# A filter product moved into an earlier slot of the interleaved order, and two of a unit's four closing sums moved one turn later

## The chip, the cores and the metric

The kernel runs on one core of a Trainium2 chip. The metric is device time in microseconds of one execution; the runs of the kernel before gave 2632.1, 2633.94 and 2633.98 us, median 2633.94.

## What is computed

A real FFT along the sequence, a product with a complex filter, the inverse FFT, and then a two-layer block with an ELU between the layers. Everything is float32.

```python
batch, seq, dim = (8, 3008, 256);  n_tokens, d_model, d_ff = (24064, 256, 2048)
X = np.fft.rfft(x, axis=1)
Y = X * (filt_r + 1j * filt_i)[None, :, :]
x = np.fft.irfft(Y, n=3008, axis=1).reshape(24064, 256)
h = x @ w_in
g = np.where(h > 0.0, h, np.exp(np.minimum(h, 0.0)) - 1.0)
return g @ w_out
```

## The kernel before

**Two workloads in one order.** The length 3008 is 47 x 64, and the FFT is done as products with small tables. Batch 0 goes through its FFT in a first stage (about the first 105 us of the span). From then on the two-layer block of batch b-1 and the FFT of batch b share the engines: the two-layer block is the base load, and the FFT's steps are put between its steps at places written out by hand.

**The two-layer block.** The tokens of a batch are cut into six units, m = 0 to 5 (512 tokens each, 448 for m = 0). The hidden width is cut into four, q = 0 to 3. One item is (batch, m, q): 192 items in all. Both matrix products of an item are made with seven block products instead of eight (a Strassen-like scheme), so that sums on VectorE stand around them. The main loop (lines 948 to 970) has one *turn* per item: turn i issues the seven "up" steps of item i (`up_steps`, line 515: x @ w_in and the ELU) interleaved with the seven "down" steps of item i-1 (`down_steps`, line 600: g @ w_out into the four PSUM tiles po0 to po3). A step is two matmuls in the program, which the profile shows as four instructions. The up steps go in the order 1, 2, 6, 5, 7, 3, 4 (`UPS`).

Four lines of the up steps matter here:

```python
def s7():
    add("b22", mm(7, "d", True), g["t4"])     # VectorE reads bank phd
...
def s4():
    add("b21", mm(4, "d", False), g["t2"])    # TensorE adds onto the same bank phd
```

Step 7 writes the PSUM bank phd, VectorE reads it in the sum "b22" (line 538), and only then may step 4 add onto the same bank. Two other steps (3, and one down step) lie between steps 7 and 4 on TensorE. In the profile step 7 is `phd<-y`, step 4 is `phd<-ys`, both at line 530, and "b22" is the first `g<-phd` of a turn at line 538. The sum "b11" is the one `g<-pha` of a turn.

**Places in a turn.** `at(turn, place, fn)` fills a plan. Place 2 stands after the third step of a turn, place 0 in the middle (after the seventh or eighth step), place 1 at the end, behind the closing sums of the turn's up item (lines 588 to 592) and, where q is 3, behind three sums of the down item (line 628). Each engine works its instructions in program order.

**The FFT of batch b** has its turns counted from t = 24(b-1); r below is the turn's number less t. Four input steps `x_unit` (four VectorE operations for a pair, lines 219 and 220) stand in place 0 of r = 0, 2, 4 (for b = 1: 2, 3, 4). Then four groups follow, with s = t + 6, 10, 14, 18: `b_unit` at s, `re_mult` and `re_sums` at s+1, `im_mult` and `im_join` at s+2 (r = 8, 12, 16, 20), `im_sums` and `bi_unit` at s+3 (r = 9, 13, 17, 21). `im_mult` (line 415) makes four 128x512 products for the filter, lines 417 and 418, once for c = 0 and once for c = 1; `im_join` (line 423) adds them; `im_sums` (line 428) makes two sums that the matmuls of `bi_unit` (line 445) read. The filter's next slices are read by `f_read` (line 323, issued by GpSimd), which waits for the last `im_mult` of the group before. `n_unit` (line 479), TensorE work that makes the two-layer block's next input, stands in place 0 of r = 8, 12, 16 and 23 and in place 1 of r = 1 and 5; r = 20 has none. The four sums behind it, `n_sums` (lines 505 to 508), stand at the end of r = 1, 5, 9, 13 and 17 and in place 0 of r = 23.

**A unit's end.** When q = 3 is done, ScalarE copies po0 and po1 (line 617), VectorE makes three sums in the turn's tail, and a list `rest` of four more sums, all at line 628, runs in `c_unit`, place 0 of r = 4m + 5. One turn later, in place 0 of r = 4m + 6, `o_unit` makes two transposes on VectorE (line 650) and issues the output's DMAs on SyncE (line 660). So `c_unit` falls on r = 5, 9, 13, 17, 21 and 25, and `o_unit` on r = 6, 10, 14, 18, 22 and 26; r = 26 is r = 2 of the next batch, whose `x_unit` pair stands in the same place behind it.

Of the kernel before, what the change touches and what calls it, by code (L numbers as in the profile page):

```python
# [130 lines left out]
def kernel(  # L131
# [51 lines left out]
    xs, tas, tns, t1s, t2s, rs, ss, t3s, t4s, zs, yds, ys, g_of, po_of, cs_, sds = ({} for _ in range(16))  # L183

    def raw(src, row, ap, col=0):
        return bass.AP(tensor=src.tensor, offset=src.offset + row * D + col, ap=ap)
# [281 lines left out]
    def half(m):  # L468

        return 224 if m == 0 else 256  # L470
# [129 lines left out]
    def down_steps(b, m, q):  # L600
        h = half(m)
        g = g_of.pop((b, m, q))
        if q == 0:
            po_of[b, m] = [psO.tile([P, 2, 256], FP32, tag="po%d" % i, name="po%d" % i) for i in range(4)]
        po = po_of[b, m]
        k = {}

        def step(n):
            i, u = PLACE[n]
            for a in range(2):  # L610

                nc.tensor.matmul(po[i][:, u, 0:h], w_out[q][:, COMBO[n], a, :], g[n][:, a, :],  # L612
                                 start=q == 0 and a == 0 and n in (1, 3, 6, 4), stop=True, skip_group_check=True)
            if q == 3 and n == 7:
                for i in range(2):
                    t = k[i] = kp.tile([P, 2, 256], FP32, tag="k%d" % i, name="k%d" % i)
                    nc.scalar.activation(out=t[:, :, 0:h], in_=po[i][:, :, 0:h], func=AXT.Copy)

        def tail():
            if q != 3:  # L620
                return
            p1, p5 = (k[0][:, u, 0:h] for u in range(2))
            p35, p7 = (k[1][:, u, 0:h] for u in range(2))
            c = kp.tile([P, 2, 512], FP32, tag="c", name="c")
            (c11, c12), (c21, c22) = ((c[:, i, 0:h], c[:, i, h:2 * h]) for i in range(2))

            def add(o, i0, i1):
                nc.vector.tensor_tensor(out=o, in0=i0, in1=i1, op=ALU.add)  # L628

            add(p35, p35, p5)  # L630
            add(c12, po[2][:, 1, 0:h], p1)
            add(c11, po[2][:, 0, 0:h], p1)
            rest = [(p7, p7, c12), (c12, c12, p35), (c21, po[3][:, 0, 0:h], p7), (c22, p7, p5)]
            cs_[b, m] = c, lambda: [add(*r) for r in rest]

        return [(lambda n=n: step(n)) for n in DOWNS], tail

# [2 lines left out]


    def c_unit(b, m):
        cs_[b, m][1]()

    def o_unit(b, m):
        c, _ = cs_.pop((b, m))
        o = op.tile([P, 16, 2, 32], FP32, tag="o", name="o")
        n = 7 if m == 0 else 8
        for k in range(2):
            nc.vector.transpose(out=o.rearrange("p (j k) e s -> p j k e s", k=2)[:, 0:n, k],  # L650
                                in_=c.rearrange("p e (j k s) -> p j k e s", k=2, s=32)[:, 0:n, k])

        o = o.rearrange("p (u f k) e s -> p u f k (e s)", u=4, f=2)
        queues = itertools.cycle((nc.sync, nc.scalar) if (b, m) == (B - 1, 5) else (nc.sync,))
        for k in range(2):
            for u, w, i in ((0, 3, 1), (3, 1, 0)) if m == 0 else ((0, 4, 4 * m),):
                for f in range(1 if i == 0 else 2):
                    n1 = N1 - i if f else i
                    for a in range(4):
                        next(queues).dma_start(raw(out, b * N + n1 + 32 * N1 * k,  # L660
                                                   [[N1 * D, 32], [-D if f else D, w], [1, 64]], 64 * a),
                                               o[ts(a, 32), u:u + w, f, k])
# [113 lines left out]
    with tc.manual_schedule():  # L776
# [118 lines left out]
        def at(quad, place, fn, *a):  # L895
            plan.setdefault((quad, place), []).append((fn, a))
# [13 lines left out]
        for b in range(B):  # L910
            t = (b - 1) * PER
            if b > 0:
                for c, s in enumerate((2, 2, 3, 3, 4, 4) if b == 1 else (0, 0, 2, 2, 4, 4)):
                    at(t + s, 0, x_unit, b, c)
                    if c % 2 == 0:
                        opens.add(t + s + 1)
                        at(t + s, 1, a_unit, b, c)
                    nb, nxt = (b, c + XBUFS) if c + XBUFS < NXC else (b + 1, c + XBUFS - NXC)
                    if nb < B:
                        at(t + s, 1, x_load, nb, nxt)  # L920
                    at(t + s, 1, z_write, b, c)
                for g in range(0, NG, 2):
                    s = t + 6 + 2 * g
                    opens.update((s + 1, s + 4))
                    for k in (g, g + 1):
                        at(s - 2, 1, f_read, b, k)
                        at(s - 1, 0, z_read, b, k)
                    at(s, 1, b_unit, b, g)
                    at(s + 1, 2, re_mult, b, g)
                    at(s + 1, 1, re_sums, b, g)  # L930
                    at(s + 2, 2, im_mult, b, g, 0)
                    at(s + 2, 1, im_mult, b, g, 1)
                    at(s + 2, 1, im_join, b, g)
                    at(s + 3, 2, im_sums, b, g)
                    at(s + 3, 1, bi_unit, b, g)
                    at(s + 3, 1, y_write, b, g)
            for m, (s, place) in enumerate(((23, 0), (25, 1), (29, 1), (32, 0), (36, 0), (40, 0))):
                if b > 0 or m > 0:
                    at(t + s - 2, 0, tn_read, b, m)
                    at(t + s - 2, 1 if m == 0 else 0, y_read, b, m)  # L940
                    at(t + s, place, n_unit, b, m)

                    at(*((t + s + 1, 1) if m > 2 else (t + s, place)), n_sums, b, m)
                at(t + PER + 4 * m + 5, 0, c_unit, b, m)
                at(t + PER + 4 * m + 6, 0, o_unit, b, m)

        items = [(b, m, q) for b in range(B) for m in range(6) for q in range(4)]
        for i in range(-PER, len(items) + 3):
# [3 lines left out]
            for n, k in enumerate("DUUDUDDU" if i in opens else "UUDUDDU"):  # L952
                s = ups if k == "U" else downs
# [7 lines left out]
            for k in "DUUDUD" if i in opens else "DUUDUDD":  # L961
                s = ups if k == "U" else downs
# [40 lines left out]
```

## Time and profile before

| what | value |
|---|---|
| median of the runs | 2633.94 us |
| the profiled execution | 2636.78 us |
| its span, first to last instruction | 2635.0 us |
| granted TensorE clock, mean | 0.992 |
| TensorE busy | 2556.2 us, 97% |
| VectorE busy | 2041.0 us, 77% |
| ScalarE busy | 1549.3 us, 59% |
| GpSimd busy | 166.2 us, 6% |
| VectorE line 628 | 288 sums, median 415 to 425 ns |
| VectorE lines 417, 418 | 56 products each, mean 691 and 683 ns |
| VectorE line 650 | 96 transposes, median 670 ns |

Time in the tables is of one profiled execution. "Busy" is the union of an engine's instructions. In a timeline's line, the first number is the start in us from the span's start, the second the duration, then engine, line, operation, out<-in and shapes; a bracket gives the idle time in front of it and what ended that. On VectorE the next instruction can start before the one in front has its end on record (starts 0.60 us apart for durations of 0.68), so costs on VectorE are taken from start to start. Matmuls overlap in the same manner: four of a step start 0.2 us apart though each is recorded with 0.38 us.

### The profile page before, as it was taken

Reading aid. Unit: us, or ns where it says so; the run is one execution under the profiler, and the core shown is the slowest. Engines: PE = TensorE matmul, PEld = TensorE weight load, DVE = VectorE, ACT = ScalarE, POOL = GpSimd, SP = SyncE. Lnnn points to the kernel's source line nnn. Section 1 sums busy time; section 2 is a strip of 40 time slices with the busy share of each in tenths; the row PEclk is TensorE's granted clock in tenths of the full one; section 3 lists DMA queues with packets and bytes.
Section 4 is the critical chain, followed back from the end, with each engine's and each line's share of the span. In section 5 each row is a group of like instructions: output and inputs, shape, how many; then the busy total and the mean of one; then the engine's idle time right before and its main releaser. Section 6 shows DMA issues by size and latency. Waiting matters only on the chain.

```text
span 2635.0 us, 39708 instructions
## 1 busy us (share of the span) xinstructions
PE 2556.2 (97%) x14460; PEld 2202.1 (84%) x14460; DVE 2041.0 (77%) x3538; ACT 1549.3 (59%) x2713; POOL 166.2 (6%) x333
## 2 busy tenths in 40 slices
PE   5799999999999999999999999999999999999998
PEld 4588879888898888988889888898888888798887
DVE  6878887788777887777877888778887788866666
ACT  6665555665556555655556555565555655555554
POOL 5100000001000100000000000000000000000000
PEclk8899999999999999999999999999999999999999
DMA  9562213522243232433215231253213322120010
GB/s 290 160 173 70 57 37 94 129 57 69 49 117 82 69 73 48 109 86 72 65 41 140 70 84 39 65 130 81 60 38 89 83 68 57 39 58 20 21 29 17
DMA packets 228834, 206.37 MB, mean 78 GB/s; under 512 B 130962, under 2 KB 194674, under 8 KB 228640
## 3 DMA queue, kind: packets, MB, share of 16 engines
q1 hardware_dynamic: 211328, 166.87, 25.8%
q0 software_dynamic: 15856, 36.25, 4.9%
q8 instruction: 114, 1.87, 0.3%
q10 hardware_dynamic: 1456, 0.72, 0.1%
q14 instruction: 80, 0.66, 0.1%
HBM read 131.87 MB, written 78.17 MB: 80 GB/s over the span
## 4 chain that ended last, share of the span: by engine, by line
PE 77%; DVE 15%; ACT 3%; issue 2%; DMA 0%; DVEq 0%; ACTq 0%
PE po L612 34%; PE phs L530 20%; PE phd L530 10%; PE pha L530 5%; PE psn L479 3%; DVE g L538 2%; DVE g L552 2%; DVE c L628 2%; PE psa L233 1%; PE pf L382 1%; DVE zs L428 1%; PE pv L445 1%; ACT e L548 1%; ACT e L547 1%; DVE g L589 1%
## 5 line engine op out<-in xcount | busy, mean ns | idle before, releaser
L612 PE MATMUL po<-g,wo 128*128 128x256 f32 (+1 forms) x5376 | 1313.4, 376 | 0.0
L612 PEld LDWEIGHTS po<-g,wo 128*128 128x128 f32 x5376 | 1013.1, 190 | 162.2 <-issue 47.4
L541 ACT ACTIVATE g<-phs 128x512 f32<-128x512 f32 (+1 forms) x576 | 338.6, 588 | 763.4 <-PE phs L530 763.3
L538 DVE TENSOR_TENSOR g<-phd,g 128x512 f32<-128x512 f32 (+1 forms) x384 | 259.6, 676 | 346.2 <-ACT e L548 228.5
L548 ACT ACTIVATE e<-e 128x512 f32<-128x512 f32 (+1 forms) x768 | 477.2, 621 | 24.3
L547 ACT ACTIVATE e<-g 128x512 f32<-128x512 f32 (+1 forms) x576 | 354.1, 615 | 84.9 <-DVE g L538 47.8
L530 PE MATMUL phs<-y,wi 128*128 128x256 f32 (+1 forms) x1536 | 389.3, 376 | 0.5
L530 PE MATMUL phs<-ys,wi 128*128 128x256 f32 (+1 forms) x1536 | 387.8, 375 | 1.5 <-ACT g L541 1.5
L552 DVE SCALAR_TENSOR_TENSOR g<-e,g 128x512 f32<-128x512 f32 (+1 forms) x576 | 387.4, 673 | 1.7 <-ACT e L548 0.2
L530 PEld LDWEIGHTS phs<-ys,wi 128*128 128x128 f32 x1536 | 291.7, 190 | 35.0 <-ACT g L541 2.2
L530 PEld LDWEIGHTS phs<-y,wi 128*128 128x128 f32 x1536 | 287.9, 190 | 38.4 <-ACT fall L390 3.4
L552 DVE SCALAR_TENSOR_TENSOR g<-e,phs 128x512 f32<-128x512 f32 (+1 forms) x192 | 129.7, 676 | 124.9 <-ACT e L548 124.9
L530 PE MATMUL phd<-ys,wi 128*128 128x256 f32 (+1 forms) x768 | 197.5, 380 | 28.7 <-DVE g L538 28.1
L530 PE MATMUL pha<-y,wi 128*128 128x256 f32 (+1 forms) x768 | 193.9, 375 | 0.0
L530 PE MATMUL phd<-y,wi 128*128 128x256 f32 (+1 forms) x768 | 193.8, 375 | 0.0
L530 PEld LDWEIGHTS phd<-ys,wi 128*128 128x128 f32 x768 | 143.0, 190 | 57.5 <-DVE g L538 42.6
L547 ACT ACTIVATE e<-phs 128x512 f32<-128x512 f32 (+1 forms) x192 | 112.8, 587 | 109.3 <-PE phs L530 109.3
L323 POOL DMA_DIRECT2D fall<-fp x224 | 110.0, 499 | 836.8 <-DVE r L418 775.1
L530 PEld LDWEIGHTS pha<-y,wi 128*128 128x128 f32 x768 | 146.3, 191 | 16.5
L530 PEld LDWEIGHTS phd<-y,wi 128*128 128x128 f32 x768 | 146.0, 190 | 16.4
L538 DVE TENSOR_TENSOR g<-pha,g 128x512 f32<-128x512 f32 (+1 forms) x192 | 129.2, 673 | 25.4 <-PE pha L530 25.3
L589 DVE TENSOR_TENSOR g<-g,g 128x512 f32<-128x512 f32 (+1 forms) x192 | 130.7, 681 | 6.7
(138 smaller groups left out, 2119.2 us busy)
## 6 DMA issues: line engine op xcount, KB each, us to landing
yd<-t SPq DMA_DIRECT2D x127, 192.0 KB
t<-yd SPq DMA_DIRECT2D x190, 128.0 KB
z<-t SPq DMA_DIRECT2D x84, 256.0 KB
fall<-fp POOLq DMA_DIRECT2D x224, 96.0 KB, 3.0
t<-z SPq DMA_DIRECT2D x224, 96.0 KB
out_dram<-o SPq DMA_DIRECT2D x632, 32.0 KB
tn<-tn_t SPq DMA_DIRECT2D x48, 256.0 KB
xc<-in_x_dram SPq DMA_DIRECT2D x84, 128.0 KB
```

What stands on the lines that cost most here:

```text
L233: nc.tensor.matmul(p[o:o + 64, u, :], w[r, u, o:o + 64], src[r, u, :], start=True, stop=True)
L323: nc.gpsimd.dma_start(t[32 * a:32 * a + 24].rearrange("p c u d -> p (c u d)"), fp[g, a].rearrange("q c u d -> q (c u d)"))
L479: nc.tensor.matmul(ps[:, ts(q, P)], t[:, i - 4 * m, ds(dh * P, P)], w[:, i - 4 * m, :], start=True, stop=True)
L530: nc.tensor.matmul(ps[:, a, 0:h], w_in[q][:, COMBO[n], a, :], y[n], start=start and a == 0, stop=True, skip_group_check=True)
L538: nc.vector.tensor_tensor(out=g[o], in0=i0, in1=i1, op=ALU.add)
L541: nc.scalar.activation(out=g[o], in_=i0, func=AXT.Copy)
L547: nc.scalar.activation(out=e, in_=src, func=AXT.Relu, scale=-1.0)
L548: nc.scalar.activation(out=e, in_=e, func=AXT.Exp, scale=-1.0)
L552: nc.vector.scalar_tensor_tensor(out=g[n], in0=es[n], scalar=1.0, in1=src, op0=ALU.subtract, op1=ALU.max)
L589: nc.vector.tensor_tensor(out=b12, in0=b22, in1=b12, op=ALU.subtract)
L612: nc.tensor.matmul(po[i][:, u, 0:h], w_out[q][:, COMBO[n], a, :], g[n][:, a, :], start=q == 0 and a == 0 and n in (1, 3, 6, 4), stop=True, ...
L628: nc.vector.tensor_tensor(out=o, in0=i0, in1=i1, op=ALU.add)
```

## The change

The list `rest` has its second and third sum exchanged, and is run in two halves: (p7, c21) stays in `c_unit`, and (c12, c22) goes to the start of `o_unit`, one turn later, in front of the transposes. `im_mult` for c = 1 moves from place 1 of its turn (the end) to place 2 (behind the third step), directly behind `im_mult` for c = 0. No instruction is added or dropped.

```diff
-            rest = [(p7, p7, c12), (c12, c12, p35), (c21, po[3][:, 0, 0:h], p7), (c22, p7, p5)]
-            cs_[b, m] = c, lambda: [add(*r) for r in rest]
+            rest = [(p7, p7, c12), (c21, po[3][:, 0, 0:h], p7), (c12, c12, p35), (c22, p7, p5)]
+            cs_[b, m] = c, lambda i: [add(*r) for r in rest[i:i + 2]]
...
     def c_unit(b, m):
-        cs_[b, m][1]()
+        cs_[b, m][1](0)
 
     def o_unit(b, m):
-        c, _ = cs_.pop((b, m))
+        c, join = cs_.pop((b, m))
+        join(2)
         o = op.tile([P, 16, 2, 32], FP32, tag="o", name="o")
...
-                    at(s + 2, 2, im_mult, b, g, 0)
-                    at(s + 2, 1, im_mult, b, g, 1)
+                    for c in range(2):
+                        at(s + 2, 2, im_mult, b, g, c)
                     at(s + 2, 1, im_join, b, g)
```

## The prediction, made before the changed kernel was run

> **What bounds the kernel now.** I read the page first, for the bound, then the list of waits, for what the bound waits for, then the timelines of TensorE and VectorE around those waits, turn by turn. Turns are named by r as above.
>
> On the page TensorE is busy 97% of the span and VectorE 77%. The page's chain of the work that ended last:
>
> ```profile
> PE 77%; DVE 15%; ACT 3%; issue 2%; DMA 0%; DVEq 0%; ACTq 0%
> ```
>
> TensorE is the bound, but 15% of the chain that ended last runs over VectorE: there are stretches in which VectorE decides when TensorE goes on. The list of waits (total us, times, longest) names the place:
>
> ```profile
> PE phd L530 <- DVE g L538: 28.1, 29, 1.4
> ```
>
> Step 4 waits for the sum b22. In the timeline of TensorE these waits are regular: in each of the seven batches 0.85 us in r = 9, 13, 17 and 1.38 us in r = 21, together 21 x 0.85 + 7 x 1.38 = 27.5 us; one of 0.6 us is left over, at 146 us. One of them, at r = 13, in TensorE's timeline:
>
> ```profile
> 1233.04 1.03 PE L530 MATMUL phd<-y,wi 128*128 128x256 f32 x4
> 1233.90 1.03 PE L530 MATMUL phs<-y,wi 128*128 128x256 f32 x4
> 1234.76 1.03 PE L612 MATMUL po<-g,wo 128*128 128x256 f32 x4
> 1236.64 1.13 PE L530 MATMUL phd<-ys,wi 128*128 128x256 f32 x4 [0.85 <-DVE g L538]
> 1237.61 1.89 PE L612 MATMUL po<-g,wo 128*128 128x256 f32 x8
> ```
>
> Steps start 0.864 us apart when nothing holds them (1233.90 to 1234.76). From 1234.76 to 1237.61 there are two steps, 1.73 us, in 2.85: the stall costs 1.12 us, more than its idle row, because overlap with the step in front is lost (0.16) and the step behind starts late too (0.11). At r = 21 the same two steps take 3.37 us (1340.84 to 1344.21): 1.64 us. VectorE in front of it, r = 12 and 13:
>
> ```profile
> 1219.95 0.68 DVE L418 TENSOR_TENSOR r<-r,fall 128x512 f32<-128x512 f32 x1
> 1222.09 0.69 DVE L538 TENSOR_TENSOR g<-phd,g 128x512 f32<-128x512 f32 x1 [1.45 <-PE phd L530]
> ...
> 1230.23 0.68 DVE L417 TENSOR_TENSOR r<-r,fall 128x512 f32<-128x512 f32 x1
> 1230.83 0.69 DVE L418 TENSOR_TENSOR r<-r,fall 128x512 f32<-128x512 f32 x1
> 1231.43 1.29 DVE L423 TENSOR_TENSOR r<-r 128x512 f32<-128x512 f32 x2
> ...
> 1234.44 0.42 DVE L628 TENSOR_TENSOR k<-k,c 128x256 f32<-128x256 f32 x1
> 1234.89 0.42 DVE L628 TENSOR_TENSOR c<-c,k 128x256 f32<-128x256 f32 x1
> 1235.23 0.42 DVE L628 TENSOR_TENSOR c<-po,k 128x256 f32<-128x256 f32 x1
> 1235.57 0.42 DVE L628 TENSOR_TENSOR c<-k,k 128x256 f32<-128x256 f32 x1
> 1235.90 0.68 DVE L538 TENSOR_TENSOR g<-phd,g 128x512 f32<-128x512 f32 x1
> ```
>
> In r = 12 VectorE idles 1.45 us in front of b22, waiting for step 7. From 1224.77 to 1235.90 it has no idle time, and b22 of r = 13 starts 2.86 us after step 7 did (1233.04). In an undisturbed turn it starts 1.135 us after step 7 (1220.95 to 1222.09), step 4 follows 2.59 us after step 7, and step 4 needs b22 0.74 us before it (1235.90 to 1236.64). So b22 may start up to 1.85 us after step 7 without any cost: that is the measure for every row below.
>
> **The product c = 1 in place 2.** It removes lines 417 and 418 from the queue ahead of r = 9, 13, 17, 21 (1230.23 to 1231.43, 1.20 us) and puts the same 1.20 us ahead of b22 in r = 8, 12, 16, 20. In r = 12 the 1.45 us of idle time covers it, and in r = 8 and 16 idle times of 1.36 and 1.45 do: cost nothing, with 0.16 us over; if the cover is gone, the slack from 1.135 to 1.85 still takes 0.7 us. r = 20 has no `n_unit` in front of step 7, and so no idle time; TensorE's timeline and then VectorE's:
>
> ```profile
> 1327.02 1.03 PE L530 MATMUL phd<-y,wi 128*128 128x256 f32 x4
> 1329.61 1.03 PE L530 MATMUL phd<-ys,wi 128*128 128x256 f32 x4
> ```
>
> ```profile
> 1327.81 0.68 DVE L418 TENSOR_TENSOR r<-r,fall 128x512 f32<-128x512 f32 x1
> 1328.41 0.68 DVE L538 TENSOR_TENSOR g<-phd,g 128x512 f32<-128x512 f32 x1
> ```
>
> b22 there starts 1.39 us after step 7 and would start 1.20 us later, at 1329.61; step 4 can then start at 1329.61 + 0.74 = 1330.35 and not at 1329.61. With the 0.11 us for the step behind, a new stall of 0.85 us, seven times: 5.9 us. The rest of r = 20 is hardly later: one of the maxima behind b22 (line 552) waits for ScalarE until 1330.78 anyway, so VectorE has caught up there, and what step 4 being late adds behind it is some 0.2 us.
>
> **The two sums one turn later.** In r = 9, 13, 17, 21 they leave the queue ahead of b22. Four sums now take 1.46 us (1234.44 to 1235.90): 0.45 for one whose successor reads its result, 0.34 for the others. The half (p7, c21) takes 0.45 + 0.34 = 0.79, so 0.67 go. In `o_unit` c12 and c22 come in front of the transposes, which read c22: 0.34 + 0.45 = 0.79 us. In r = 6, 10, 14, 18, 22 VectorE idles between 2.44 and 4.14 us in front of b22 (3.77 at 1195.57): covered. In r = 2 the `x_unit` pair stands behind the transposes, and b22 is late already (a timeline of both engines):
>
> ```profile
> 1088.77 0.62 DVE L538 TENSOR_TENSOR g<-phd,g 128x448 f32<-128x448 f32 x1
> 1089.44 1.02 PE L530 MATMUL phd<-ys,wi 128*128 128x224 f32 x4
> ```
>
> b22 has no idle time in front of it, it starts as soon as the last operation of the pair lets it (line 220, 1088.16), and step 4 starts 1.00 us after the step in front (1088.44), where 0.756 is its spacing with 224 columns. Any delay there is paid in full: 0.79 us, in the six batches (b = 2 to 7) in which the output of a unit m = 5 meets an `x_unit` pair: 4.7 us. The 13 or so output DMAs of a unit are issued on SyncE 0.79 us later as well. Behind them in SyncE's queue stand table, input and x loads for turns to come, and the list of that queue's waits shows it waiting for producers, 1002 us in line 456 alone: nothing.
>
> **One rule weighed.** A sum whose successor reads it takes 0.45 us from start to start and the others 0.34 (the four rows of line 628 above), and I use both. The Trainium skill, "VectorE: DVE Perf Modes", section "The DRAIN you can't avoid", says that a semaphore between chained VectorE operations adds nothing. By that rule c12 and c22 would cost 0.68 us in r = 2 and not 0.79, and the gain would be 0.7 us larger; the row goes against the rule, by 0.11 us, and I keep the row.
>
> **What is late next.** With both edits b22 of r = 9, 13, 17 reaches the head of VectorE's queue 2.86 - 1.20 - 0.67 = 0.99 us after step 7, before its data: it starts at 1.135, and step 4 doesn't wait. With the product alone it would be 1.66, still under 1.85. In r = 21, 3.40 - 1.20 - 0.67, less the 0.85 that TensorE is later by and plus 0.2: 0.98; also clear. The other input of b22, t4, is made by ScalarE at 1232.38 to 1232.98 in r = 13, 1.2 us before it is wanted. `f_read` on GpSimd waits for line 418 and so starts some 9 us sooner, and takes 3.9 us of descriptor work; at its place now (1231.81) the VectorE operations beside it keep 0.68 us, and its transfers land in 3.0 us, some two turns before `re_mult` reads them: nothing.
>
> **Sum.** 21 x 1.12 + 7 x 1.64 = 35.1 us of stalls go; 5.9 (r = 20) and 4.7 (r = 2) come. Net 24.4 us. From the profiled 2636.8 us (span 2635.0 and 1.8 around it) this gives 2612.4; the median of the runs is 2.8 us below the profiled one, so **2609.5 us** is forecast, 0.93% less. A measurement tells 0.2% (5.3 us) from no change.
>
> **Unknown costs and the rivals.** (a) *The stalls are only worth their idle rows.* Ends of matmuls are modelled, so the spacing may overstate what returns. Then 27.5 us go, and 7 x 0.57 (1330.35 less 1329.78, the end of the step in front) and 6 x 0.79 come: 18.7 us, 2615.2. Against it: the spacing of starts is not modelled. (b) *The new stalls don't come*, because VectorE reaches b22 sooner than its rows say: up to 35.1 us, 2599 us; r = 20 alone gone, 2603.5. Against it: both places have zero idle time on VectorE in front of b22 now. (c) *Slower.* In r = 9, 13, 17, 21 step 4 could find b22 held by its other input, t4 from ScalarE, as late as VectorE's queue makes it now; then nothing is won, and the 10.7 us of r = 20 and r = 2 are paid: 2644.6. It decides from the point at which ScalarE's copy ends 2.9 us later than it does (1232.98 to 1235.90). ScalarE is idle 2 us in front of that copy, waiting for TensorE, which speaks against it. (d) *Nothing changes*, since the sums and products reach VectorE in another order than the program's or wait for something not shown: 2634.
>
> Chances: forecast 0.76, (a) 0.12, (b) 0.07, (c) 0.03, (d) 0.02. So faster 0.95, same 0.02, slower 0.03. The range takes in (a), and of (b) the case without the stall in r = 20, with about 1.5 us on either side for the drift between runs (the runs of before differ by 1.9): 2602 to 2617.
>
> **What would show it.** The list of waits should give step 4 for b22 at about 10 us instead of 28.1: seven of 0.57 in r = 20, six of 0.9 in r = 2, the one at 146 us. At r = 13 the four steps from 7 to 4 should be evenly 0.864 apart, with b22 1.135 us after step 7; r = 20 should take 12.9 us instead of 12.1. The prediction is wrong in its mechanism if a wait of another engine stands in front of step 4 in r = 13, or of line 445 behind it, and in its sizes if r = 8, 12 or 16 stalls too.

## The result, and the profile after

The changed kernel takes 2609.81 us (median of 4 runs, 2608.95 to 2612.41) beside 2633.37 us before (4 runs): a ratio of 0.9913, 95% interval 0.9896 to 0.993. That is 23.6 us less; 2609.5 us and 24.4 us less were forecast. The profiled execution took 2609.69 us with a span of 2607.9 us.

The page's chain, and the wait of step 4 for b22 in the list of waits of the changed kernel:

```profile
PE 89%; DVE 6%; DMA 2%; ACT 1%; issue 1%; POOL 0%; DVEq 0%; ACTq 0%; POOLq 0%
```

```profile
PE phd L530 <- DVE g L538: 10.0, 14, 0.9
```

VectorE's share of the chain fell from 15% to 6%, and the wait from 28.1 us in 29 places to 10.0 us in 14: "about 10 us, seven of 0.57, six of 0.9, the one at 146 us" was the expectation. TensorE's timeline of r = 13 in the same batch as before:

```profile
1219.01 1.03 PE L530 MATMUL phd<-y,wi 128*128 128x256 f32 x4
1219.87 1.03 PE L530 MATMUL phs<-y,wi 128*128 128x256 f32 x4
1220.74 1.03 PE L612 MATMUL po<-g,wo 128*128 128x256 f32 x4
1221.60 1.03 PE L530 MATMUL phd<-ys,wi 128*128 128x256 f32 x4
1222.46 1.89 PE L612 MATMUL po<-g,wo 128*128 128x256 f32 x8
```

Steps 7 to 4 and the one behind stand 0.86 us apart with no bracket, where 1.12 us were lost. VectorE's timeline of r = 12 and 13:

```profile
1206.53 0.68 DVE L417 TENSOR_TENSOR r<-r,fall 128x512 f32<-128x512 f32 x1
1207.13 0.68 DVE L418 TENSOR_TENSOR r<-r,fall 128x512 f32<-128x512 f32 x1
1208.06 0.69 DVE L538 TENSOR_TENSOR g<-phd,g 128x512 f32<-128x512 f32 x1 [0.25 <-PE phd L530]
...
1219.21 0.41 DVE L628 TENSOR_TENSOR k<-k,c 128x256 f32<-128x256 f32 x1
1219.65 0.42 DVE L628 TENSOR_TENSOR c<-po,k 128x256 f32<-128x256 f32 x1
1220.14 0.69 DVE L538 TENSOR_TENSOR g<-phd,g 128x512 f32<-128x512 f32 x1
```

The idle time in front of b22 of r = 12 went from 1.45 to 0.25 us, by the 1.20 us of the two products, and b22 itself starts as it did, 1.13 us after step 7. In r = 13 two sums are left in front of b22, which now starts 1.13 us after step 7 (1219.01 to 1220.14) and not 2.86. The bill is in the other two places. r = 20, TensorE and then VectorE:

```profile
1310.76 1.03 PE L530 MATMUL phd<-y,wi 128*128 128x256 f32 x4
...
1314.10 1.13 PE L530 MATMUL phd<-ys,wi 128*128 128x256 f32 x4 [0.58 <-DVE g L538]
1315.07 1.89 PE L612 MATMUL po<-g,wo 128*128 128x256 f32 x8
```

```profile
1312.76 0.68 DVE L418 TENSOR_TENSOR r<-r,fall 128x512 f32<-128x512 f32 x1
1313.36 0.69 DVE L538 TENSOR_TENSOR g<-phd,g 128x512 f32<-128x512 f32 x1
```

And r = 2, in a timeline of all engines:

```profile
1071.23 0.41 DVE L628 TENSOR_TENSOR c<-c,k 128x256 f32<-128x256 f32 x1
1071.56 0.42 DVE L628 TENSOR_TENSOR c<-k,k 128x256 f32<-128x256 f32 x1
1072.01 1.30 DVE L651 STREAM_TRANSPOSE o<-c 128x512 f32<-128x512 f32 x2
...
1075.86 0.62 DVE L538 TENSOR_TENSOR g<-phd,g 128x448 f32<-128x448 f32 x1
...
1076.53 1.02 PE L530 MATMUL phd<-ys,wi 128*128 128x224 f32 x4 [0.88 <-DVE g L538]
```

In r = 20 b22 starts 2.60 us after step 7 and step 4 waits; in r = 2 the two sums take 0.33 and 0.45 us in front of the transposes, and the wait of step 4 grows from 0.09 to 0.88 us.

A turn's length, from the start of one step 1 to that of the next, gives the same account for one batch (the fourth; the others agree within 0.1 us, but for the first, whose r = 0 to 4 hold other work):

| turn r | before, us | after, us | difference |
|---|---|---|---|
| 2 | 13.79 | 14.59 | +0.80 |
| 9 | 15.49 | 14.37 | -1.12 |
| 13, 17 | 15.33 | 14.22 | -1.11 each |
| 20 | 12.09 | 12.94 | +0.85 |
| 21 | 15.87 | 14.22 | -1.65 |
| all others | | | 0 |

The whole main loop can be read from the view of the tile phs, which gives the shortest, median and longest ns, then the first and the last start. The first start is that of step 1 in the first turn, the last one belongs to step 3 in the last turn. Before and after:

```profile
L530 PE MATMUL phs<-y,wi x1536: 352/379/582, 102.9 to 2616.9; 128*128 128x256 f32 x160, 128*128 128x224 f32 x32
```

```profile
L530 PE MATMUL phs<-y,wi x1536: 352/379/581, 100.4 to 2589.7; 128*128 128x256 f32 x160, 128*128 128x224 f32 x32
```

2514.0 us became 2489.3: 24.7 us less, where 24.4 were forecast (each start is rounded to 0.1 us). Of these, 0.27 us lie in the loop's very first turn (7.42 and 7.15 us), which the edits don't touch and which takes between 6.98 and 7.56 us in the ten profiles; the turns of the table, summed over all batches, became 24.3 us shorter. The start of the loop, 102.9 and 100.4 us, isn't the change's: the first stage is the same program in all kernels here, and its end lies between 97.7 and 104.3 us in the ten profiles. That spread is larger than most of what the experiments tell apart, so below each kernel is judged by its loop, with the medians beside it.

### The profile page after: what moved, and what is told of

Read it like the earlier page. It is cut to its first block, busy times and chain, and to the rows that moved or that the text cites. A ratio compares the mean times of both kernels' runs of the same rounds, so it can differ in the third digit from the quotient of the medians.

```text
span 2607.9 us, 39668 instructions
## 1 busy us (share of the span) xinstructions
PE 2549.2 (98%) x14460; PEld 2204.1 (85%) x14460; DVE 2046.0 (78%) x3538; ACT 1546.1 (59%) x2713; POOL 169.6 (7%) x333
## 4 chain that ended last, share of the span: by engine, by line
PE 89%; DVE 6%; DMA 2%; ACT 1%; issue 1%; POOL 0%; DVEq 0%; ACTq 0%; POOLq 0%
PE po L612 41%; PE phs L530 23%; PE phd L530 12%; PE pha L530 6%; PE psn L479 3%; PE psa L233 1%; PE pf L382 1%; PE pv L445 1%; DVE g L538 1%; DVE g L552 1%; DMA fd<-in_filt_i_dram 1%; DMA t<-in_moe_w_out_dram 0%; ACT e L548 0%; ACT e L547 0%; DMA fd<-in_filt_r_dram 0%
## 5 line engine op out<-in xcount | busy, mean ns | idle before, releaser
L548 ACT ACTIVATE e<-e 128x512 f32<-128x512 f32 (+1 forms) x768 | 477.2, 621 | 24.4
L530 PEld LDWEIGHTS phs<-ys,wi 128*128 128x128 f32 x1536 | 291.4, 190 | 35.4 <-ACT g L541 2.5
```

The lines of the kernel that those rows point to most:

```text
L530: nc.tensor.matmul(ps[:, a, 0:h], w_in[q][:, COMBO[n], a, :], y[n], start=start and a == 0, stop=True, skip_group_check=True)
L548: nc.scalar.activation(out=e, in_=e, func=AXT.Exp, scale=-1.0)
```

## The experiments

The theory is the prediction's: a turn loses time only if b22 starts too late after step 7, each place by itself. The first rival is that stalls shrink with the work taken out of the queue; others stand with each run. Times of the kernel before in the two sets of runs: 2633.24 us (9 runs) and 2634.7 us (6 runs).

**The product alone.** The sums stay together:

```diff
-                    at(s + 2, 2, im_mult, b, g, 0)
-                    at(s + 2, 1, im_mult, b, g, 1)
+                    for c in range(2):
+                        at(s + 2, 2, im_mult, b, g, c)
```

> Only the product c = 1 is moved to place 2; the four closing sums stay together in c_unit. Theory of the prediction (a threshold: b22 may start up to 1.85 us after step 7 at no cost): b22 of r = 9, 13, 17 starts 2.86 - 1.20 = 1.66 us after step 7, that of r = 21 at about 1.7, all under the threshold, so all 35.1 us of old stalls go; r = 20 keeps its new stall of 0.85 us (5.9 us); r = 2 is as before. Net 29.2 us below the kernel before, 2604.2 us, so 4.7 us below the changed kernel. Rival (the stalls shrink in proportion to the work that is taken out of the queue, 1.20 us of the 1.87 us by the product and 0.67 by the sums): 0.64 of 35.1 less 5.9, 16.6 us below before, 2616.8 us, slower than the changed kernel.

Measured: 2606.14 us (4 runs), ratio 0.9895 (0.9881 to 0.9908). The loop is 28.2 us shorter than before (99.5 to 2585.3), so by the loop the product alone wins more than both edits together (by the medians it isn't clear, since the intervals of the two ratios overlap). b22 starts 1.66 us after step 7 in r = 13 and 17 and 1.64 in r = 21, and these turns take 14.22 us, not one hundredth more than with both edits. The proportional rival is out. One row is off: r = 9 takes 14.55 us in six batches of the seven, 0.18 more than with both edits, since b22 starts there at 1.94 and not at 1.66; that is 1.1 us in all, and makes up the difference between 29.2 and 28.2. In the other batch b22 starts at 1.74 and the turn takes 14.37 us. The rows of step 4 in the six slower turns show no idle time in front of it, so the list of waits doesn't show this loss; the turn's length does. Its cause is looked for below.

**The sums alone.** The list is split as in the change, and the product c = 1 stays at the end of its turn:

```diff
+            rest = [(p7, p7, c12), (c21, po[3][:, 0, 0:h], p7), (c12, c12, p35), (c22, p7, p5)]
+            cs_[b, m] = c, lambda i: [add(*r) for r in rest[i:i + 2]]
...
                     at(s + 2, 2, im_mult, b, g, 0)
                     at(s + 2, 1, im_mult, b, g, 1)
```

> Only the four closing sums are split and half of them moved behind; the product c = 1 stays at the end of its turn. Threshold theory: b22 of r = 9, 13, 17 starts 2.86 - 0.67 = 2.19 us after step 7 and that of r = 21 at 3.40 - 0.67 = 2.73, over 1.85, so each of the 28 stalls only shrinks by 0.67 us (18.8 us), no stall in r = 20, and r = 2 pays 6 x 0.79 = 4.7 us. Net 14.0 us below before, 2619.4 us. Together with the product alone that would be 43 us, far more than the 24 us of both: the two edits pay for the same stalls. Rival (in proportion, effects add up): 0.36 of 35.1 less 4.7, 7.9 us below before, 2625.5 us.

Measured: 2620.97 us (5 runs), ratio 0.995 (0.9938 to 0.9963); loop 14.4 us shorter. b22 starts 2.20 us after step 7 in r = 9, 13, 17 and 2.73 in r = 21, and in r = 13 TensorE's timeline keeps a shorter stall:

```profile
1225.88 1.13 PE L530 MATMUL phd<-ys,wi 128*128 128x256 f32 x4 [0.18 <-DVE g L538]
```

The turn takes 14.67 us, 0.66 less than before, where 0.67 us of work were taken out. The two edits alone win 28.2 and 14.4 us, together 24.7: they pay for the same stalls, and in the changed kernel the sums add only their own cost in r = 2, apart from r = 9.

**Both edits, but not for a batch's last unit.**

```diff
         cs_[b, m][1](0)
+        if m == 5:
+            cs_[b, m][1](2)
...
-        join(2)
+        if m < 5:
+            join(2)
```

> Both edits, but the last unit of a batch (m = 5) keeps its four sums together in c_unit. Theory: only r = 2 differs from the changed kernel, where b22 has no slack; 6 x 0.79 = 4.7 us less than the changed kernel, 2604.2 us, 29.2 below before, and the four steps in r = 2 are as before. Rival (r = 2 is late by its own x_unit pair, and the sums in front of it are absorbed elsewhere): no difference from the changed kernel, 2609.

Measured: 2603.27 us (4 runs), ratio 0.988 (0.9867 to 0.9894); loop 29.6 us shorter than before. r = 2 is back at 13.80 us, and every other turn is as in the changed kernel: the 4.7 us of the change in r = 2 are shown to come from the two sums in front of the `x_unit` pair.

**The product behind b22.** On top of the last one, a place 3 behind step 7 takes the product c = 1:

```diff
-                        at(s + 2, 2, im_mult, b, g, c)
+                        at(s + 2, 2 + c, im_mult, b, g, c)
...
-            for k in "DUUDUD" if i in opens else "DUUDUDD":
+            for n, k in enumerate("DUUDUD" if i in opens else "DUUDUDD"):
...
+                if n == 1:
+                    for fn, a in plan.get((i, 3), ()):
+                        fn(*a)
```

> As the one without m = 5, and the product c = 1 is issued not in front of b22 but right behind step 7's two VectorE operations (b22 and the maximum of b11), where VectorE waits for ScalarE 0.79 us in r = 8, 12, 16 and 1.08 us in r = 20 before the next maximum. Theory: r = 20 loses its new stall of 0.85 us; of the 1.20 us of products 0.41 us (0.12 in r = 20) stays in the queue, so b22 of r = 9, 13, 17 comes to the head of the queue 2.86 - 0.79 - 0.67 = 1.40 us after step 7 and in r = 21 at 3.40 - 1.08 - 0.67 = 1.65, all under 1.85: no stall is left but the old one in r = 2, 35.1 us below before, 2598.3 us. Rival (what is put behind b22 delays the maxima and closing sums, and the down steps of the next turn wait for those): new waits of the down steps or of step 2 in r = 9, 13, 17, 21 of 0.4 us each, 28 x 0.4 = 11 us, 2609 us.

Measured: 2600.35 us (4 runs), ratio 0.9869 (0.9854 to 0.9884); loop 35.4 us shorter. VectorE's timeline of r = 20:

```profile
1309.20 0.69 DVE L538 TENSOR_TENSOR g<-phd,g 128x512 f32<-128x512 f32 x1
1309.80 0.69 DVE L552 SCALAR_TENSOR_TENSOR g<-e,g 128x512 f32<-128x512 f32 x1
1310.40 0.69 DVE L417 TENSOR_TENSOR r<-r,fall 128x512 f32<-128x512 f32 x1
1311.00 0.69 DVE L418 TENSOR_TENSOR r<-r,fall 128x512 f32<-128x512 f32 x1
1311.60 0.69 DVE L552 SCALAR_TENSOR_TENSOR g<-e,phs 128x512 f32<-128x512 f32 x1
```

The products fill the time in which VectorE waited for ScalarE between two maxima. r = 20 takes 12.09 us again, and b22 starts 1.31 us after step 7 in r = 13 and 1.57 in r = 21 (1.40 and 1.65 were expected). No later step waits for it; the rival with 11 us of new waits is out.

**One sum more.** The product alone, with an extra sum in front of b22, to find the bound:

```diff
-(c22, p7, p5)]
+(c22, p7, p5)] + 1 * [(p5, p5, p1)]
```

> The product moved alone, and one sum more (p5 = p5 + p1, read by nobody) at the end of c_unit, 0.34 us in VectorE's queue in front of b22. The runs so far fit one line: what a turn loses is the start of b22 after step 7 less 1.75 us, and nothing below that (2.20 gave 0.45, 2.60 gave 0.84, 2.73 gave 0.98, 2.86 gave 1.11, 3.40 gave 1.64; 1.66 gave 0; 1.94 gave 0.18). By that line b22 of r = 13 starts at 1.66 + 0.34 = 2.00 and the turn takes 14.22 + 0.25 = 14.47 us, r = 17 the same, r = 21 at 1.98 takes 14.45; the prediction's own bound, 1.85 with 0.11 us for the step behind, gives 0.26. Rival: the bound is 1.85 and the 0.11 us belong to long stalls alone, 14.37.

Measured in one run: 2622.04 us; the loop is 16.6 us shorter than before. VectorE's rows in r = 13:

```profile
1228.33 0.42 DVE L628 TENSOR_TENSOR c<-k,k 128x256 f32<-128x256 f32 x1
1228.78 0.43 DVE L628 TENSOR_TENSOR k<-k 128x256 f32<-128x256 f32 x1
1229.12 0.68 DVE L538 TENSOR_TENSOR g<-phd,g 128x512 f32<-128x512 f32 x1
```

The sum cost 0.46 us and not 0.34, since it writes what the one in front reads and so waits for it (0.45 from 1228.33 to 1228.78, 0.34 for the next). b22 starts at 2.12 us, and the turn takes 14.59: 0.37 lost, which is 2.12 less 1.75. In r = 9 2.40 lost 0.65, in r = 21 2.10 lost 0.35. So the line holds at three more points, and the expected size was wrong by the cost of the sum. The rival (1.85 without the 0.11) would give 0.27 in r = 13 and is out.

**Without GpSimd's copies, and with twice as many.** The product alone, with line 431 left out, and made twice:

```diff
-        if g == 0:
-            for c in range(2):
-                nc.gpsimd.tensor_copy(out=z[0:32, 2 + c, 0, :], in_=t[0:32, 1 - c, 0, :])
```

```diff
-            for c in range(2):
+            for c in (0, 1, 0, 1):
                 nc.gpsimd.tensor_copy(out=z[0:32, 2 + c, 0, :], in_=t[0:32, 1 - c, 0, :])
```

> The product moved alone, and GpSimd's two copies of line 431 left out (the four rows with the special factors of the first group then hold the sums of line 428, so that part of the result is left undone). In the run of the product alone these copies, 1.26 us in r = 9, lay beside the first two sums of c_unit, which took 0.62 and 0.50 us instead of 0.42, and b22 started 1.94 us after step 7 and not 1.66. Theory (the copies slow VectorE's sums with two operands in SBUF): without them the sums take 0.42, b22 starts at 1.66 and r = 9 takes 14.37 us instead of 14.55. Rival (r = 9 is slow for another reason, such as the filter's transfers, which now land sooner): 14.55 as before.

> The product moved alone, and GpSimd's two copies of line 431 made twice, 2.5 us in a row in r = 9. Theory: they now lie beside all four sums of c_unit in r = 9. The first, second and fourth read two operands in SBUF and are slowed by 0.1 to 0.2 us each; the third and b22 read one from PSUM and one from SBUF and, if only the second SBUF operand is slowed, keep their time. b22 starts at about 2.1 us after step 7, and r = 9 takes 14.37 + 0.35 = 14.7 us. Rival (GpSimd isn't the cause): 14.55.

r = 9 in a timeline of all engines with the product alone, then with the copies twice:

```profile
1163.28 1.26 POOL L431 COPY zs<-r 32x256 f32<-32x256 f32 x2 [6.70 <-DVE zs L428]
...
1163.66 0.62 DVE L628 TENSOR_TENSOR k<-k,c 128x256 f32<-128x256 f32 x1
...
1164.32 0.50 DVE L628 TENSOR_TENSOR c<-c,k 128x256 f32<-128x256 f32 x1
...
1164.74 0.41 DVE L628 TENSOR_TENSOR c<-po,k 128x256 f32<-128x256 f32 x1
```

```profile
1161.71 2.13 POOL L431 COPY zs<-r 32x256 f32<-32x256 f32 x4 [6.71 <-DVE zs L428]
1162.09 0.62 DVE L628 TENSOR_TENSOR k<-k,c 128x256 f32<-128x256 f32 x1
1162.74 0.50 DVE L628 TENSOR_TENSOR c<-c,k 128x256 f32<-128x256 f32 x1
1163.17 0.41 DVE L628 TENSOR_TENSOR c<-po,k 128x256 f32<-128x256 f32 x1
1163.50 0.62 DVE L628 TENSOR_TENSOR c<-k,k 128x256 f32<-128x256 f32 x1
```

Without the copies the four sums take 0.42 to 0.43 us, b22 starts at 1.66 and r = 9 takes 14.37 us (2602.49 us in one run, loop 29.3 us shorter, the 29.2 of the prediction's theory). With the copies twice (2604.32 us in one run, loop 27.3 us shorter) the fourth sum is slowed too, the third with its operand in PSUM is not, b22 starts at 2.15 and the turn takes 14.77 in four batches; in the other three b22 starts at 1.95 and the turn takes 14.57. GpSimd's copies are the cause, and the filter's transfers aren't.

In those three batches, and in the one batch of the product alone with b22 at 1.74, it is the copies that are longer, while the first sum keeps 0.42 us. That batch of the product alone:

```profile
1790.75 1.29 DVE L428 TENSOR_TENSOR zs<-r 128x512 f32<-128x512 f32 x2
1791.57 1.59 POOL L431 COPY zs<-r 32x256 f32<-32x256 f32 x2 [6.71 <-DVE zs L428]
1791.95 0.42 DVE L628 TENSOR_TENSOR k<-k,c 128x256 f32<-128x256 f32 x1
```

The pair of copies takes 1.59 us and not 1.26, though it starts as long ahead of the first sum (0.38 us) as in the other six.

**No stall in r = 2.** On top of the product behind b22, the last unit's transposes go to the end of their turn:

```diff
-                at(t + PER + 4 * m + 6, 0, o_unit, b, m)
+                at(t + PER + 4 * m + 6, 1 if m == 5 and b < B - 1 else 0, o_unit, b, m)
```

> As the run with the product behind b22, and the transposes and output DMAs of the units m = 5 stand at the end of r = 2 and not in its middle, so that the x_unit pair is in front of b22 alone. VectorE's queue in r = 2 is 1.22 us shorter in front of b22, which was 1.85 us after step 7 with 224 columns and comes down to 1.03; the 0.35 us that r = 2 loses go, six times: 2.1 us below that run, 13.44 us for the turn instead of 13.79, and 37 us below before, 2596 us. Rival (the transposes at the end of r = 2 hold the closing sums' successors, the first sum of r = 3): 0.3 us come back in r = 3 (9.84 us now), no gain.

Measured: 2598.44 us (4 runs) beside 2634.7, ratio 0.9863 (0.9846 to 0.9881). Loop 37.4 us shorter than before, r = 2 at 13.44 us, r = 3 unchanged at 9.84. The medians don't tell it from the kernel with the product behind b22 (intervals overlap); the turn's length does. In this kernel step 4 waits for b22 only once, 0.64 us near the loop's start.

## Why the prediction was right, step by step

- *The sum* came out term by term, not by errors that cancel. Over all batches the stalls that went were 34.9 us (35.1 forecast), r = 20 cost 5.9 (5.9) and r = 2 cost 4.7 (4.7). That the median fell within 0.3 us of the forecast is luck: the end of the first stage alone moves by 6.6 us between the profiles.
- *The stalls in r = 9, 13, 17 and 21* were sized at 1.12 and 1.64 us by the spacing of steps; the turns became 1.11 to 1.12 and 1.65 us shorter. Rival (a), which took only the idle rows (0.85 and 1.38), is out.
- *The cover in r = 8, 12, 16* held: these turns are 13.87 us in both kernels, with 0.14 to 0.25 us of idle time left.
- *r = 20* was forecast at 0.85 us and measured at 0.85; *r = 2* at 0.79 and measured at 0.80. Rival (b) is out.
- *What is late next:* nothing, as forecast. Rival (c), the other input of b22, showed up in no row, and (d) is out with the order of VectorE's rows.
- *The rule weighed:* the sum that feeds the transposes takes 0.45 us from start to start and the one in front 0.33, so the row was right against the rule, and the extra sum of the experiment showed the same 0.45.
- *The bound for b22*, "up to 1.85 us without any cost", was mis-sized. In a turn with 256 columns what is lost is b22's start after step 7 less 1.75 us, within 0.02 us, at eleven different starts from 1.94 to 3.40 us, and one start at 1.74 lost nothing; the 0.11 us that I had added for the step behind are this same difference. For the sum it made no difference, since every stall in it was beyond both.
- *f_read's earlier start at "nothing"* failed in a small part. The prediction looked at `f_read` on GpSimd, but not at the two copies of line 431 that stand behind it in GpSimd's queue in r = 9. They used to run after the descriptor work, beside the last sum and b22; now they start as soon as their input is there, beside the first sums. In the changed kernel that makes b22 of r = 9 start at 1.19 us and not at 1.135, at no cost; with the product alone it cost 0.18 us in six batches of the seven.
- *The sums' edit* was taken as a part of the gain. By the runs it is none: the product alone takes down all the 28 stalls but for 0.18 us in six of them, and the sums bring 4.7 us of loss in r = 2 and 1.1 us of gain in r = 9. The prediction had the row for it (1.66 under the bound) and didn't draw the conclusion. That 1.66 is under the bound as measured too is a matter of 0.09 us.

The profiled pair differs by 27.1 us, more than the 24.7 of the loop; 2.5 us of that are the first stage's end.

## What to carry to other kernels

On an engine that is nearly always busy, measure for each wait how late its release comes after the earliest moment it could, and what lateness is free; moving work in front of a release costs only what goes beyond that, and taking more away than the lateness wins nothing. Look for idle time of the engine that is moved to behind the release, and not only in front of it: the same work that cost 0.85 us in front of b22 in r = 20 cost nothing 1.2 us later. A move that helps 28 places can lose at one where another batch's work happens to share the slot, so list all places that the edited line runs in.

## What the runs showed of the hardware

On VectorE, a 128x256 float32 sum takes 0.45 us from start to start when its successor depends on it, by a read of its result or (in the run with one sum more) by a write onto its input, and 0.34 us when it doesn't.

A copy on GpSimd (32 partitions by 256, both ends in SBUF) and a 128x256 float32 sum on VectorE with two operands in SBUF lengthened one another: in r = 9 the first sum took 0.62 us instead of 0.42, or else the pair of copies took 1.59 us instead of 1.26 (it took 0.84 in the kernel before). A sum with an operand in PSUM stayed at 0.41 us beside them. The Trainium skill, "SBUF — State Buffer", section "Who interferes with whom", states that a VectorE operation with two inputs in SBUF contends with a GpSimd instruction that reads SBUF, and that the order of issue decides who waits. The rows agree on the contention: with the copies twice it cost 0.20 us for two of the three sums that it applies to and 0.08 for the third. In the kernel before, a sum with two SBUF operands that started 0.17 us ahead of the copies kept 0.42 us. The order of the recorded starts didn't decide it, though: the copies started 0.38 us ahead of the first sum in both outcomes. A reason that fits, and that no run tests, is that the first copy was itself still waiting: the second sum of line 428, which also has two operands in SBUF, started 0.22 us ahead of it. On the other hand 3.9 us of descriptor work on GpSimd lengthened none of the VectorE operations beside it.
